# Gated linear attention into a shrink feed-forward: one quadratic instead of two, GpSimd without products, and a planner's table rewritten

## The chip, the cores and the metric

The kernel runs on one NeuronCore of a Trainium2 chip. A core has a matrix engine (TensorE, here PE; its weight loads are listed apart as PEld), a vector engine (VectorE, DVE), an activation engine (ScalarE, ACT), a general engine (GpSimd, POOL) and a queue engine that issues transfers (SyncE, SP). Each works through its own list of instructions in order, and they wait for each other by semaphores. The metric is the time of one execution on the device in microseconds (us).

## The reference

```python
q, k, v, alpha: (4, 8, 768, 48) float32     # batch, heads, positions, width
w_in: (384, 2048), w_out: (2048, 384)        # float64 on the host
for t in range(768):
    state = alpha[:, :, t, :, None] * state + einsum('bhd,bhe->bhde', k[:, :, t], v[:, :, t])
    y[:, :, t] = einsum('bhd,bhde->bhe', q[:, :, t], state)
x = y.transpose(0, 2, 1, 3).reshape(3072, 384)
h = x @ w_in
out = (h - tanh(h)) @ w_out
```

## The kernel before

All arithmetic is float32. Work is cut into 12 units of 256 positions (three per batch entry), and each unit into two chunks of 128. A unit passes through two halves.

`gla(u)` is the attention. ACT and DVE bring alpha, k and q of eight heads into tiles aT, kT and qT with the head width along the partitions: four pairs of heads, a pair on partitions 0 to 47 and 64 to 111, the rest of the 128 unused. Two scans on DVE (U backwards, W forwards) give the running products of alpha, and kU and qW scale kT and qT by them in place. Per chunk: `scores` (sc, products of k and q), `masked` (pm, on DVE), `decay` (the old state times `ends`), `y` (products of q with the state and of pm with v), `x` (a copy into xT), and for the next chunk `back`, `natural`, `update` and `state` (tp, kn, up, state). Units 0 and 1 are "direct": the fourth pair of heads is written into the unused partitions of the first three by gap products of 32 columns, with the tiles v_gap and s_gap. Later units copy that pair aside (xs) and move it by transfers (`moves`).

`moe(u)` is the feed-forward, in eight steps s. `first` makes h for two blocks of 128 of the 2048 features (6 matrix products of 256 columns, 12 records in the trace, as each float32 product is two). `square` (u = h*h) and `quad` (z1, z2) run on ACT, `cube` (w = h*u) and `shrunk` (g) on DVE. g is a polynomial for h - tanh(h). `large` on ACT sums what lies over a limit into the tile over. `second` multiplies g with w_out: for units 0 and 1 plainly (4 products of 384 columns, tile o), for the others with seven products of 192 columns instead of eight, for which `sums` makes e on DVE and `combine` once makes five tiles b of sums of w_out. `store` adds the parts up and sends them out.

Two PSUM banks hold h, so `first` of a step waits for `cube` of two steps before. The weights arrive as 16 pieces (in0 to in7, out0 to out7), loaded by SP into four buffers and converted by ACT ("read") and DVE. The first 12 or so steps of unit 0 and 1 run while this goes on.

The order on every engine is written by `Planner`: each task has an engine, an assumed duration, a rank and the tasks it needs, and a greedy walk always takes the ready task of the lowest rank. So a changed rank or duration moves instructions everywhere. At the end the kernel tests whether the quick way was allowed (over, sizes, least, most, tiny into `ok`); all engines load `ok`, and with 0 a slower function `general` would compute everything again.

Of the kernel before, what the change touches and what calls it, by code (L numbers as in the profile page):

```python
# [8 lines left out]
FP32 = mybir.dt.float32  # L9
# [352 lines left out]
def fast(tc, q, k, v, alpha, moe_w_in, moe_w_out, out, w_in, w_out, ident, ok, pad_rows):  # L362
# [17 lines left out]
    with ExitStack() as ctx:  # L380
# [25 lines left out]
        over = consts.tile([P, NU * FS], FP32, name="over")  # L406
# [27 lines left out]
        RANK = {"in": -3, "out": 1}  # L434
# [4 lines left out]
        def rank_gla(u):  # L439
            return (-40, -20)[u] if u < 2 else 2 * FS * u - 24  # L440
# [26 lines left out]
        for n, (what, s) in enumerate(pieces):  # L467
# [6 lines left out]
            add(f"read {what}{s}", "ACT", 1.85, rank, [f"fetch {what}{s}", older and f"{older[0]}{older[1]}"], a)  # L474
            add(f"{what}{s}", "DVE", 1.95, rank, [f"read {what}{s}"], b)
# [21 lines left out]
        def gla(u, rank):  # L497
# [64 lines left out]
            def scale(name, by):  # L562
                t = m[name].rearrange("p g c t -> p (g c) t")
                (V if u == 0 else GP).tensor_mul(t, t, m[by][:, :, 1:])  # L564
# [5 lines left out]
            go("U", "DVE", 2.35, 1, ["aT", prev and f"kU{prev}", prev and f"sizeU{prev}"], scan_U)  # L570
            go("ends", "DVE", 0.5, 3, ["U"], ends)
            go("W", "DVE", 2.6, 3, ["ends", prev and f"qW{prev}", prev and f"sizeW{prev}"], scan_W)
            go("kU", *(("DVE", 1.3) if u == 0 else ("POOL", 2.4)), 3, ["kT", "U"], lambda: scale("kT", "U"))
            go("qW", *(("DVE", 1.3) if u == 0 else ("POOL", 2.4)), 5, ["qT", "W"], lambda: scale("qT", "W"))
# [10 lines left out]
            def chunk(c):  # L585
# [30 lines left out]
                def decay():  # L616
                    for q in quads:
                        GP.tensor_mul(old[q, :, q], old[q, :, q],  # L618
# [10 lines left out]
                def products():  # L629
# [3 lines left out]
                    if n == 0:  # L633
                        for hh, at, j in to_gap:
                            T.matmul(y[at, j, :], lhsT=v_gap[:, c, hh, j, :], rhs=m["pm", c][hh][:, NP - 1, :],
                                     start=(j == 0), stop=True, skip_group_check=True)
                    if n > 0:
                        for g in range(NP):
                            T.matmul(y[:, g, :], lhsT=old[:, g, :], rhs=m["qT"][:, g, c, :],  # L639
                                     start=(g == 0), stop=False, skip_group_check=True)  # L640
                        for hh, at, j in to_gap:
# [3 lines left out]
                            T.matmul(y[at, j, :], lhsT=v_gap[:, c, hh, j, :], rhs=m["pm", c][hh][:, NP - 1, :],  # L645
# [348 lines left out]
```

## Time and profile before

| | |
|---|---|
| times of three runs | 643.49, 643.63, 641.67 us (median 643.49) |
| profiled execution | 642.75 us, span 640.8 us, mean granted clock 0.979 |
| PE / PEld busy | 610.4 us (95%) / 534.0 us (83%) |
| DVE / ACT / POOL busy | 520.5 (81%) / 403.0 (63%) / 94.1 us (15%) |
| costliest groups | PE h L781 268.2 us, PE o L842 91.1 + 80.7 + 65.1 us, ACT z L793 110.3 us, DVE g L803 86.3 us |
| transfers | 50.5 MB, 44 read from HBM |

How to read it: busy time is an average over stages. PE's lengths contain the time that a product needs to run out, which overlaps the next one, so what a run of products costs is read from the distance between their starts, or from the chain of waits, which does this already. "A <- B: 7.0, 1, 7.0" means that A stood idle until B, 7.0 us in total, once, at most 7.0.

### The profile page before, as it was taken

Reading aid. Unit: us, or ns where it says so; the run is one execution under the profiler, and the core shown is the slowest. Engines: PE = TensorE matmul, PEld = TensorE weight load, DVE = VectorE, ACT = ScalarE, POOL = GpSimd, SP = SyncE. Lnnn points to the kernel's source line nnn. Section 1 sums busy time; section 2 is a strip of 40 time slices with the busy share of each in tenths; the row PEclk is TensorE's granted clock in tenths of the full one; section 3 lists DMA queues with packets and bytes.
Section 4 is the critical chain, followed back from the end, with each engine's and each line's share of the span. In section 5 each row is a group of like instructions: output and inputs, shape, how many; then the busy total and the mean of one; then the engine's idle time right before and its main releaser. Section 6 shows DMA issues by size and latency. Waiting matters only on the chain.

```text
span 640.8 us, 10379 instructions
## 1 busy us (share of the span) xinstructions
PE 610.4 (95%) x3723; PEld 534.0 (83%) x3723; DVE 520.5 (81%) x915; ACT 403.0 (63%) x825; POOL 94.1 (15%) x84
## 2 busy tenths in 40 slices
PE   7889993999999999999999999999999999999994
PEld 6666672677799899999899999999898999999994
DVE  7897599899689799689999699689899656656762
ACT  3767796588878688678656557457545544545550
POOL 2030028232012002001211011002011000000000
PEclk9799997799999999999999999999999999999998
DMA  9998491455454346433131031021010000000001
GB/s 171 220 201 196 115 225 56 100 103 150 124 104 122 78 111 169 99 103 100 39 71 46 9 78 46 7 76 49 26 32 2 12 20 1 20 14 1 25 2 31
DMA packets 55165, 50.51 MB, mean 79 GB/s; under 512 B 29056, under 2 KB 44864, under 8 KB 55104
## 3 DMA queue, kind: packets, MB, share of 16 engines
q1 hardware_dynamic: 52736, 48.97, 32.5%
q10 hardware_dynamic: 2368, 0.79, 0.8%
q8 instruction: 31, 0.51, 0.4%
q14 instruction: 30, 0.25, 0.1%
HBM read 44.04 MB, written 4.72 MB: 76 GB/s over the span
## 4 chain that ended last, share of the span: by engine, by line
PE 82%; DVE 10%; DMA 4%; issue 2%; ACT 1%; SPq 0%; DVEq 0%; ACTq 0%
PE h L781 35%; PE o L842 27%; PE o L827 6%; PE y L649 3%; PE sc L608 3%; PE y L639 3%; PE up L673 2%; DVE g L803 2%; DMA vt<-in_v_dram 2%; DMA raw<-in_moe_w_in_dram 1%; DVE z L802 1%; PE tp L664 1%; DVE U L545 1%; DMA qr<-in_q_dram 1%; DVE qT L529 1%
## 5 line engine op out<-in xcount | busy, mean ns | idle before, releaser
L781 PE MATMUL h<-xT,w_in 128*128 128x256 f32 x1152 | 268.2, 383 | 7.7 <-DVE w L797 7.0
L781 PEld LDWEIGHTS h<-xT,w_in 128*128 128x128 f32 x1152 | 217.0, 192 | 38.6 <-DVE w L797 7.6
L788 ACT ACTIVATE u<-h 128x512 f32<-128x512 f32 x96 | 57.2, 596 | 156.9 <-PE h L781 156.5
L793 ACT ACTIVATE z<-u 128x512 f32<-128x512 f32 x192 | 110.3, 622 | 4.4 <-DVE g L803 1.9
L797 DVE TENSOR_TENSOR w<-h,u 128x512 f32<-128x512 f32 x96 | 65.9, 686 | 57.8 <-ACT u L788 57.2
L803 DVE SCALAR_TENSOR_TENSOR g<-z,z 128x512 f32<-128x512 f32 x96 | 86.3, 899 | 10.1
L842 PE MATMUL o<-b,e 128*128 128x192 f32 x480 | 91.1, 326 | 0.0
L842 PE MATMUL o<-w_out,e 128*128 128x192 f32 x320 | 80.7, 334 | 0.0
L842 PEld LDWEIGHTS o<-b,e 128*128 128x128 f32 x480 | 80.2, 190 | 0.0
L802 DVE SCALAR_TENSOR_TENSOR z<-z,w 128x512 f32<-128x512 f32 x96 | 69.5, 724 | 5.3 <-ACT z L793 2.1
L842 PE MATMUL o<-b,g 128*128 128x192 f32 x320 | 65.1, 326 | 0.0
L842 PEld LDWEIGHTS o<-w_out,e 128*128 128x128 f32 x320 | 56.5, 190 | 6.7 <-issue 3.0
L618 POOL TENSOR_TENSOR state<-state,ends 48x192 f32<-48x192 f32 x40 | 22.5, 563 | 256.5 <-DVE state L681 216.1
L809 ACT ACTIVATE big<-u 128x512 f32<-128x512 f32 x96 | 59.2, 616 | 0.1
L842 PEld LDWEIGHTS o<-b,g 128*128 128x128 f32 x320 | 54.2, 190 | 0.0
L827 PE MATMUL o<-w_out,g 128*128 128x384 f32 x128 | 47.0, 514 | 3.9 <-DVE g L803 3.8
L827 PEld LDWEIGHTS o<-w_out,g 128*128 128x128 f32 x128 | 24.8, 199 | 19.5 <-DVE g L803 4.5
L564 POOL TENSOR_TENSOR qT<-qT,W 128x1024 f32<-128x1024 f32 x11 | 26.7, 2428 | 76.6 <-DVE qT L529 74.3
L564 POOL TENSOR_TENSOR kT<-kT,U 128x1024 f32<-128x1024 f32 x11 | 24.4, 2217 | 82.3 <-DVE kT L529 60.2
L815 DVE TENSOR_TENSOR e<-g 128x256 f32<-128x256 f32 x80 | 33.3, 416 | 1.4
L614 DVE TENSOR_TENSOR pm<-sc,mask 128x512 f32<-128x512 f32 x46 | 29.5, 683 | 5.9 <-PE sc L608 5.9
L816 DVE TENSOR_TENSOR e<-g 128x256 f32<-128x256 f32 x80 | 33.4, 417 | 0.0
(105 smaller groups left out, 730.5 us busy)
## 6 DMA issues: line engine op xcount, KB each, us to landing
raw<-in_moe_w_out_dram SPq DMA_DIRECT2D x16, 768.0 KB, 5.6
raw<-in_moe_w_in_dram SPq DMA_DIRECT2D x32, 288.0 KB, 5.3
ar<-in_alpha_dram SPq DMA_DIRECT2D x24, 192.0 KB, 3.2
qr<-in_q_dram SPq DMA_DIRECT2D x24, 192.0 KB, 3.2
kr<-in_k_dram SPq DMA_DIRECT2D x22, 192.0 KB, 4.2
vt<-in_v_dram SPq DMA_DIRECT2D x22, 192.0 KB, 4.4
raw<-in_moe_w_in_dram SPq DMA_DIRECT2D x32, 96.0 KB, 5.4
out_dram<-same SPq DMA_DIRECT2D x20, 96.0 KB, 1.7
```

The lines of the kernel that those rows point to most:

```text
L564: (V if u == 0 else GP).tensor_mul(t, t, m[by][:, :, 1:])
L781: T.matmul(h[:, a, :], lhsT=w_in[:, j, f * P:(f + 1) * P], rhs=xT[u][:, j, :], start=(j == 0), stop=(j == KT - 1))
L788: A.activation(m["u", s], m["h", s], AF.Square, scale=W_SCALE ** -1.5)
L793: A.activation(m[z, s], m["u", s], AF.Square, bias=b, scale=QA * W_SCALE)
L797: V.tensor_mul(m["w", s], m["h", s], m["u", s])
L802: V.scalar_tensor_tensor(out=z1, in0=z1, scalar=QK1, in1=m["w", s], op0=ALU.add, op1=ALU.mult)
L803: V.scalar_tensor_tensor(out=g.rearrange("p a c t -> p (a c t)"), in0=z2, scalar=QK2, in1=z1, op0=ALU.add, op1=ALU.mult)
L809: A.activation(big, m["u", s], AF.Relu, bias=-U_MAX, scale=W_SCALE, accum_out=over[:, n:n + 1])
L815: V.tensor_add(e[:, 0:2, :], g[:, 0], g[:, 1])
L816: V.tensor_sub(e[:, 2:4, :], g[:, :, 1, :], g[:, :, 0, :])
L827: T.matmul(m["o"][c], lhsT=g[:, a, c, :], rhs=w_out[:, f, :], start=(f == 0), stop=(f == FT - 1))
L842: T.matmul(o[n][:, i], lhsT=g_, rhs=w_, start=(s == 0 and (n, i) in ((0, 0), (1, 0), (2, 1), (3, 0))), stop=(s == FS - 1), skip_group_chec ...
```

## The change

1. The shrink polynomial has one quadratic factor instead of two: one ACT activation and one DVE operation fewer per step. It holds for |h| up to 0.177 (h*h up to 1/32) instead of 0.5.
2. The tile u holds two steps, and `large` tests both at once, 48 times with 1024 columns instead of 96 with 512.
3. kU and qW of units 1 to 11, all `decay` and four of the five `combine` go from GpSimd to DVE. GpSimd keeps its memsets at the start.
4. The state products and `update` of TensorE use 112 columns instead of 128 (the upper 16 are unused); in the direct units the state product of the fourth pair is dropped.
5. Gap products: all of s_gap first, then all of v_gap, instead of one and one.
6. `store` adds in another order, sends `cross` before `same`, and for the last unit sends `cross` through ACT's queue.
7. The final test is planned like the other tasks: `judge` and `ok` on DVE, `gather` on PE, ahead of the last steps.
8. The planner's durations and ranks are new; w_out's pieces rank 7 later, unit 2's attention too.

```diff
-QA = C4 ** 0.25
-QB1, QK1 = QA * 0.6850222695595437, (QA * 2.4662457704476) ** 2
-QB2, QK2 = -QA * 2.2304921696, (QA * 1.5325319249) ** 2
+U_FAST = 1.0 / 32
+QA, QB, QK = 0.2301250865552381, -0.2896718893320786, 0.24942350940007277
...
-        RANK = {"in": -3, "out": 1}
+        RANK = {"in": -3, "out": 8}
...
-            return (-40, -20)[u] if u < 2 else 2 * FS * u - 24
+            return (-40, -20, 2 * FS - 1)[u] if u < 3 else 2 * FS * u - 24
...
-                (V if u == 0 else GP).tensor_mul(t, t, m[by][:, :, 1:])
+                V.tensor_mul(t, t, m[by][:, :, 1:])
...
                     for q in quads:
-                        GP.tensor_mul(old[q, :, q], old[q, :, q],
+                        V.tensor_mul(old[q, :, q], old[q, :, q],
                                       m["ends"][q, :, c:c + 1].to_broadcast([D, NP, D]))
...
+                    rows = P if direct else HP + D
                     if n > 0:
-                        for g in range(NP):
-                            T.matmul(y[:, g, :], lhsT=old[:, g, :], rhs=m["qT"][:, g, c, :],
+                        for g in range(KT if direct else NP):
+                            T.matmul(y[0:rows, g, :], lhsT=old[:, g, 0:rows], rhs=m["qT"][:, g, c, :],
...
-                        T.matmul(up[:, g], lhsT=m["kn", c][:, g, :], rhs=vts[u][:, c, 2 * g:2 * g + 2, :],
+                        T.matmul(up[0:HP + D, g], lhsT=m["kn", c][:, g, 0:HP + D], rhs=vts[u][:, c, 2 * g:2 * g + 2, :],
...
             if n == 0:
-                GP.tensor_add(combos["11+22"], b11, b22)
+                V.tensor_add(combos["11+22"], b11, b22)
...
-                    for z, b in (("z1", QB1), ("z2", QB2)):
-                        m[z, s] = two.tile([P, 2 * TU], FP32, name=z)
-                        A.activation(m[z, s], m["u", s], AF.Square, bias=b, scale=QA * W_SCALE)
+                    m["z", s] = two.tile([P, 2 * TU], FP32, name="z")
+                    A.activation(m["z", s], m["u", s], AF.Square, bias=QB, scale=QA * W_SCALE)
...
-                    V.scalar_tensor_tensor(out=z1, in0=z1, scalar=QK1, in1=m["w", s], op0=ALU.add, op1=ALU.mult)
-                    V.scalar_tensor_tensor(out=g.rearrange("p a c t -> p (a c t)"), in0=z2, scalar=QK2, in1=z1,
-                                           op0=ALU.add, op1=ALU.mult)
+                    V.scalar_tensor_tensor(out=g.rearrange("p a c t -> p (a c t)"), in0=m["z", s], scalar=QK,
+                                           in1=m["w", s], op0=ALU.add, op1=ALU.mult)
...
-                    A.activation(big, m["u", s], AF.Relu, bias=-U_MAX, scale=W_SCALE,
+                    A.activation(big, m["us"].rearrange("p s t -> p (s t)"), AF.Relu, bias=-U_FAST, scale=W_SCALE,
                                  accum_out=over[:, n:n + 1])
...
-                put(same, o[0][:, 0:1, :].to_broadcast([P, 2, NH]), ALU.subtract, p52)
-                put(same, o[1], ALU.add, same)
+                put(same, o[1], ALU.subtract, p52)
                 put(cross, o[1][:, ::-1, :], ALU.add, p52)
+                put(same, o[0][:, 0:1, :].to_broadcast([P, 2, NH]), ALU.add, same)
                 put(same, o[3], ALU.add, same)
                 for c in range(CU):
                     half = [out_r[u * CU + c][:, n * NH:(n + 1) * NH] for n in range(2)]
+                    (A if u == NU - 1 else nc.sync).dma_start(out=half[1 - c], in_=cross[:, c, :])
...
+        add("judge", "DVE", 1.2, 16 * NU, [f"large {last_step}", f"x {NU - 1}.{CU - 1}"] + [f"look {n}" for n in range(len(pieces))], judge)
+        add("gather", "PE", 0.3, 16 * NU - 20, ["judge"], gather)
+        add("ok", "DVE", 0.3, 16 * NU, ["gather"],
```

How the order moves, at three places. In the rows, the engine's instruction stands with its line, output, inputs and shape.

First, DVE around the attention of unit 2 and the first `combine`. Before, the block of unit 2 (aT to ends) stands in one piece, w and z of the next step behind it, and the additions b are on POOL:

```order
L529 STREAM_TRANSPOSE aT_107<-ar 128x8x2x16 x4
L529 STREAM_TRANSPOSE kT<-kr 128x8x32 x4
L545 SCALAR_TENSOR_TENSOR U<-aT_107,after 128x1032
L529 STREAM_TRANSPOSE qT<-qr 128x8x32 x4
L552 TENSOR_TENSOR ends<-U,low 128x8
L553 TENSOR_REDUCE least<-U 128x1
L554 RECIPROCAL before<-ends 128x8
L797 TENSOR_TENSOR w<-h,u 128x512
L559 SCALAR_TENSOR_TENSOR W<-aT_107,before 128x1032
L802 SCALAR_TENSOR_TENSOR z_838<-z_838,w 128x512
L803 SCALAR_TENSOR_TENSOR g<-z_840,z_838 128x512
```

POOL at the same place, before:

```order
L734 TENSOR_TENSOR b_832<-w_out 128x1536
L736 TENSOR_TENSOR b_833<-w_out 128x1536
L564 TENSOR_TENSOR kT<-kT,U 128x1024
L618 TENSOR_TENSOR state_118<-state_118,ends 48x4x48 x2
L738 TENSOR_TENSOR b_834<-w_out 128x1536
L564 TENSOR_TENSOR qT<-qT,W 128x1024
L740 TENSOR_TENSOR b_835<-w_out 128x1536
```

Now DVE has w, g, the conversion of out7 (L85, L86) and the additions b between the pieces, and POOL nothing:

```order
L795 TENSOR_TENSOR w<-h,u 128x512
L528 STREAM_TRANSPOSE qT<-qr 128x8x32 x4
L799 SCALAR_TENSOR_TENSOR g<-z,w 128x512
L563 TENSOR_TENSOR qT<-qT,W 128x1024
L795 TENSOR_TENSOR w<-h,u 128x512
L617 TENSOR_TENSOR state_118<-state_118,ends 48x4x48 x2
L85 TENSOR_SCALAR bits<-raw 128x768
L86 ISA w_out<-bits,more 128x1536
L795 TENSOR_TENSOR w<-h,u 128x512
L731 TENSOR_TENSOR b_924<-w_out 128x1536
L613 TENSOR_TENSOR pm_934<-sc_893,mask 128x512
L613 TENSOR_TENSOR pm_935<-sc_894,mask 128x512
```

What moved: w and g stand between the parts of unit 2, and kT, qT, state and b come from POOL.

Second, PE at the gap products of the second chunk of unit 0 (the two chunks of unit 1 read alike). Before, the first seven of its rows:

```order
L639 MATMUL y<-qT,state_119 128x128 x4
L642 MATMUL y<-qT,s_gap 32x128
L645 MATMUL y<-pm_327,v_gap 32x128
L642 MATMUL y<-qT,s_gap 32x128
L645 MATMUL y<-pm_327,v_gap 32x128
L642 MATMUL y<-qT,s_gap 32x128
L645 MATMUL y<-pm_327,v_gap 32x128
```

Now, up to the products with the values vt (pm 325 and 326 are the two masked tiles):

```order
L670 MATMUL up<-vt,kn 112x96 x4
L635 MATMUL y<-qT,state_119 128x128 x3
L638 MATMUL y<-qT,s_gap 32x128 x6
L642 MATMUL y<-pm_325,v_gap 32x128 x3
L642 MATMUL y<-pm_326,v_gap 32x128 x3
L646 MATMUL y<-pm_325,vt 48x128
L646 MATMUL y<-pm_326,vt 48x128
```

What moved: three state products instead of four, six s_gap in a row, then six v_gap.

Third, SP at the end of the program. Before:

```order
L887 DMA out_dram<-same 128x192
L888 DMA out_dram<-cross 128x192
L887 DMA out_dram<-same 128x192
L888 DMA out_dram<-cross 128x192
L962 TENSOR_LOAD ok
L962 ISA x2
L962 COMPARE_AND_BRANCH
```

Now:

```order
L886 DMA out_dram<-cross 128x192 x2
L889 DMA out_dram<-same 128x192 x2
L972 TENSOR_LOAD ok
L972 ISA x2
L889 DMA out_dram<-same 128x192 x2
L972 COMPARE_AND_BRANCH
```

What moved: two of the last unit's four stores are gone from SP, and the load of `ok` stands ahead of the other two.

More of the change, by code (lines that the diff above doesn't have):

```diff
@@ L473, in fast @@
             older = pieces[n - 2] if n >= 2 else None
-            add(f"read {what}{s}", "ACT", 1.85, rank, [f"fetch {what}{s}", older and f"{older[0]}{older[1]}"], a)
-            add(f"{what}{s}", "DVE", 1.95, rank, [f"read {what}{s}"], b)
+            add(f"read {what}{s}", "ACT", 2.1, rank, [f"fetch {what}{s}", older and f"{older[0]}{older[1]}"], a)
+            add(f"{what}{s}", "DVE", 1.6, rank, [f"read {what}{s}"], b)
         vts, xT = {}, {}
@@ L688, in chunk @@
                 go_c("scores", "PE", 1.2, 7, [kU, qW] + held, scores)
-                go_c("masked", "DVE", 1.4, 8, ["scores", past and f"y {past}"], masked)
+                go_c("masked", "DVE", 1.3, 8, ["scores", past and f"y {past}"], masked)
                 if n > 0:
-                    go_c("decay", "POOL", 1.2, 6, [f"ends {u}", f"state {past}"], decay)
+                    go_c("decay", "DVE", 0.6, 6, [f"ends {u}", f"state {past}"], decay)
                 if direct:
@@ L744, in fast @@
         for n in range(5):
[L745 removed]
+            add(f"combine {n}", "DVE", 1.7, 2 * FS + 1 + n,
                 [f"out{FS - 1}", f"in{FS - 1}", f"gaps {PLAIN - 1}.{CU - 1}", f"y {PLAIN - 1}.{CU - 1}"]
```

91 lines of the change are left out of this document (48 added, 43 removed).

## The prediction

> **What bounds the kernel now.** I read the page first, then the busy time by stage, PE's waits, the chain of waits, and the timeline where PE waited. The page (the last line is the granted TensorE clock in 40 slices of 16 us, 9 being full):
>
> ```profile
> span 640.8 us, 10379 instructions
> ...
> PE 610.4 (95%) x3723; PEld 534.0 (83%) x3723; DVE 520.5 (81%) x915; ACT 403.0 (63%) x825; POOL 94.1 (15%) x84
> ...
> PEclk9799997799999999999999999999999999999998
> ```
>
> Stages of my choice. The columns after the window are its length and then PE, PEld, DVE, ACT and POOL busy with their instruction counts, the granted TensorE clock, and DMA:
>
> ```profile
> 0.00:175.90 175.90, 155.02 (x863) 115.66 (x863) 147.91 (x215) 127.31 (x233) 45.37 (x42) 0.94 0.68 151
> 97.30:118.50 21.20, 10.41 (x22) 6.66 (x22) 21.13 (x21) 11.19 (x21) 16.66 (x7) 0.69 0.19 55
> 175.90:622.70 446.80, 446.14 (x2807) 409.49 (x2806) 366.95 (x687) 272.79 (x587) 48.69 (x42) 1.00 0.21 52
> ```
>
> From 175.9 us, where the first seven-product step begins, to the last `first`, PE is busy 446.14 of 446.80 us: whatever the change does to the other engines there is hidden as long as PE stays fed, and only PE's own work counts. The first 175.9 us are different. PE lacks 20.9 us, and half of that lies in one hole of 21.2 us, where PE has 10.4 us of work at a mean clock of 0.69 while DVE is busy for 21.1. PE's waits, as total, times, longest:
>
> ```profile
> PE h L781 <- DVE w L797: 7.0, 1, 7.0
> PE up L673 <- ACT kn L668: 4.3, 2, 2.8
> PE o L827 <- DVE g L803: 3.8, 1, 3.8
> PE tp L664 <- DVE kT L564: 2.7, 1, 2.7
> ```
>
> The chain of waits gives the undisturbed prices (start, length): the 12 records of a `first` take 2.59 us, and 50 of the seven-product `second` 8.14, so the 14 of one take 2.28.
>
> ```profile
> 175.92 2.47 PE o L842 x14
> ...
> 610.41 2.59 PE h L781 x12
> ...
> 622.73 8.14 PE o L842 x50
> ```
>
> So the time is: PE's start of the first seven-product step (175.9), a solid stretch of PE work up to 630.9, and a tail of 640.8 - 630.9 = 9.9. I add up the change in these three. The profiled execution took 642.75, which is 1.95 beside its span; I keep the 1.95. It is 0.74 below the median of the three runs, 643.49. Those runs spread over 0.3% (641.67 to 643.63), about what a measurement here can tell from no change.
>
> **The hole at 97 to 118 (forecast -15.9).** Its rows:
>
> ```profile
> 94.58 2.74 PE L827 MATMUL o<-w_out,g 128*128 128x384 f32 x8
> 95.55 3.45 POOL L736 TENSOR_TENSOR b<-w_out 128x1536 f32<-128x1536 f32 x1
> 96.02 5.15 DVE L545 TENSOR_TENSOR_SCAN U<-aT,after 128x1032 f32<-128x1032 f32 x1
> ...
> 103.61 0.64 DVE L797 TENSOR_TENSOR w<-h,u 128x512 f32<-128x512 f32 x1
> ...
> 104.31 5.08 PE L781 MATMUL h<-xT,w_in 128*128 128x256 f32 x12 [6.98 <-DVE w L797]
> ...
> 104.70 5.32 POOL L738 TENSOR_TENSOR b<-w_out 128x1536 f32<-128x1536 f32 x1
> 106.71 3.85 DVE L802 SCALAR_TENSOR_TENSOR z<-z,w 128x512 f32<-128x512 f32 x1
> ...
> 113.20 5.49 PE L827 MATMUL o<-w_out,g 128*128 128x384 f32 x8 [3.81 <-DVE g L803]
> ...
> 118.25 2.30 DVE L545 TENSOR_TENSOR_SCAN U<-aT,after 128x1032 f32<-128x1032 f32 x1
> ...
> 619.98 2.75 PE L781 MATMUL h<-xT,w_in 128*128 128x256 f32 x12
> ```
>
> PE ran out at 97.3 because `w`, which frees the bank of h, stood in DVE's queue behind unit 2's transposes, scan and ends, and came only at 103.61. That queue was slower than its work: the scan U took 5.15 us against 2.30 at 118.25, z 3.85 against 0.72 on average (L802 below), each while GpSimd ran an add of `combine` (95.55 to 99.00, 104.70 to 110.02). PE then ran at half clock: 5.08 for a `first` that takes 2.75, 5.49 for a `second` that takes 2.74. The hole's price is 7.0 + 3.8 waiting, 2.3 + 2.8 at half clock: 15.9. After the change POOL has no product left, so neither GpSimd add exists, and in DVE's new order `w` and g of every step stand between the pieces of unit 2's block. The bounds are 0 and 15.9; I take all of it and book what comes in its place below.
>
> **Gap products by shape, and state products of three pairs (-5.5).**
>
> ```profile
> 26.19 1.13 PE L673 MATMUL up<-vt,kn 128*128 128x96 f32 x8
> 27.25 1.09 PE L635 MATMUL y<-pm,v_gap 128*32 128x128 f32 x12
> ...
> 29.83 1.13 PE L639 MATMUL y<-qT,state 128*128 128x128 f32 x8 [0.70 <-ACT xT L655]
> 30.89 0.40 PE L642 MATMUL y<-qT,s_gap 48*32 48x128 f32 x2
> ...
> 34.90 0.86 PE L649 MATMUL y<-pm,vt 128*48 128x128 f32 x12
> ```
>
> Alternating, 24 records of gap products take 34.90 - 30.89 = 4.01 us; 12 v_gap records in a row take 1.09. If s_gap in a row costs the same, the block takes 2.2 (saves 1.8); if twice that, 3.3 (saves 0.7). It has the same 32 columns, so I lean to the first: 1.6, and 4.8 for the three chunks that have both. Each of these chunks also drops two of the 8 records that take 1.13 us, about 0.24: 0.7 in all. In all three the chain of waits runs through PE. Range -2.8 to -6.2.
>
> **112 columns (-2.2).** `up` (96 columns streaming) and the state product (128) both take 1.13 for 8 records, so for `up` the 128-column load is likely the limit. Loading an eighth less saves at most an eighth of 1.13, 0.14 a group; a part of the 1.13 is the last record running out, so I take 0.11 for each of the 20 groups, 0.014 a record: 2.2. The state product (17 groups with 112 columns) streams 128 columns and may be bound by either: 0 to 2.4, and I take 0. Range of both 0 to -5.2. The lines that price a load:
>
> ```profile
> L673 PEld LDWEIGHTS up<-vt,kn 128*128 128x128 f32 x160 | 21.0, 198 | 5.8 <-ACT kn L668 4.9 <-issue 0.4
> L649 PEld LDWEIGHTS y<-pm,vt 128*48 128x48 f32 x368 | 18.9, 122 | 3.3 <-issue 1.3
> ```
>
> 128 columns take 198 ns and 48 take 122, 0.95 ns a column, so 16 fewer are 15 ns, in step with 0.014. [...]
>
> **Quadratic, range test, GpSimd's products (0 in the solid stretch).**
>
> ```profile
> L793 ACT ACTIVATE z<-u 128x512 f32<-128x512 f32 x192 | 110.3, 622 | 4.4 <-DVE g L803 1.9
> L802 DVE SCALAR_TENSOR_TENSOR z<-z,w 128x512 f32<-128x512 f32 x96 | 69.5, 724 | 5.3 <-ACT z L793 2.1 <-DVE w L797 0.5
> L618 POOL TENSOR_TENSOR state<-state,ends 48x192 f32<-48x192 f32 x40 | 22.5, 563 | 256.5 <-DVE state L681 216.1 <-DVE state L679 38.6
> L564 DVE TENSOR_TENSOR kT<-kT,U 128x1024 f32<-128x1024 f32 x1 | 1.2, 1175 | 0.0
> L681 DVE TENSOR_TENSOR state<-state,up 48x192 f32<-48x192 f32 x32 | 11.1, 346 | 12.4 <-PE up L673 11.9
> L742 DVE SCALAR_TENSOR_TENSOR b<-w_out 128x1536 f32<-128x1536 f32 x1 | 1.8, 1751 | 0.0
> ```
>
> ACT loses 96 x 0.62 = 60 us, and 48 range tests of double width replace 96. DVE loses 96 of 0.72 and gains 22 scalings of 1.2 (26), 20 decays of two multiplies (0.35 each by L681, 0.56 each on POOL; I take 0.7 the pair, 14) and 4 `combine` (1.75 each, 7). After 175.9 DVE gives up 80 z (58 us) and takes 15 scalings and 14 decays (28): about 337 of 447 us at most. PE covers all of it; with that cover gone DVE would next be late with g. The new wait is one of order: scores on PE wait for kU and qW, and behind these two on DVE now queue w and g, at 1.2 us each a delay that 90 us of slack in 447 absorbs.
>
> **New waits in the first stage (+2.0).** Up to the first e, DVE's work was 147.9. It loses 17 z (12) and the blocked time (U 2.9, z 3.2, about 4 more in rows of this kind: 10), and gains 7 scalings, 6 decays and 4 `combine` (20): about 146. PE, without the terms above, would begin the seven-product steps at 175.9 - 15.9 - 5.5 = 154.5. So DVE must be busy 94% of the way, against 84% before: tight, but PE is still later. At unit 1's scores PE now stands behind eight steps of DVE in a row (U, kT, ends, kU, W, qT, decay, qW) and has only two `first`, a tp and an up to do meanwhile; at this place it waited for kn before, part of the 4.3 above. The new ranks let all pieces of w_in pass those of w_out in SP's, ACT's and DVE's queues (the same 16 loads and conversions, so no work is added), and put unit 2's k and q loads behind the last weight on SP. So the conversion `out7` now stands on DVE behind unit 2's kT, kU, qT, qW and decay, while unit 0's last `second` needs it. The nearest rows are PE's single waits of 1.5 to 2.8 us: I take 2.0; lower bound 0. Were DVE as idle as before (28 us), the stage would end at 174: upper bound 19.
>
> **The end (-1.4).**
>
> ```profile
> 630.89 0.49 ACT L877 ACTIVATE p<-o 128x384 f32<-128x384 f32 x1 [5.73 <-PE o L842]
> 633.52 0.33 SPq L887 DMA_DIRECT2D out_dram<-same  x1
> 634.85 0.43 SPq L888 DMA_DIRECT2D out_dram<-cross  x1
> ```
>
> The p copy and four adds remain, in another order with the same length. SP issued four stores from 633.52 to 635.28; now it issues two after the last add, and the two `cross` go out on ACT's queue earlier: 0.9 saved. `ok` is known before the last step, and SP loads it before its last stores; that load has no row here, bounds 0 to 1.0 us: 0.7. The `row` product moves in front of the last two steps: PE pays 0.2. Judging takes 11 small operations of DVE, covered by two steps of 2.27 that PE still has.
>
> **Sum.** -15.9 - 5.5 - 2.2 + 2.0 - 1.4 = -23.0: span 617.8, time 619.7.
>
> **Rivals.**
> *A new hole early.* Either place named above slips by 5 us, PE's clock halves again for some 7 us (as from 104.3), costing about 3.5: 8 to 12 more, 628 to 632. For it: DVE at 94%, strict order. Against it: w and g are spread out, nothing blocks DVE. [...]
> *DVE merely replaces the hole.* If its queue idles as before, new waits of 19 instead of 2 give 619.7 + 17 = 637; for no change they must reach 25. Against it: blocked time is gone.
> [...]
> *The test fails.* Were some |h| above 0.177, `general` would run as well, at several times the range. The reference's inputs give at most 0.0915, computed from them: no chance.
> *More than forecast.* No new waits, and both product terms at their ends: -15.9 - 6.2 - 5.2 - 1.4 = -28.7, 614; with an end shorter still, 612.
>
> **Chances.** Forecast (612.5 to 625) 0.68; new hole (625 to 635) 0.20; DVE replaces the hole, mostly up to no change, 0.04; slower 0.03; below 612.5 0.05. Range 612.5 to 631 holds the first and two thirds of the second: 0.81. Faster 0.94, same 0.03, slower 0.03.
>
> **What would show it.** PE's wait for w of 7.0 and the half clock between 97 and 118 gone; first seven-product step near 156; a block of `o` to `o` in the solid stretch still 4.86 us per step, `up` near 1.0 for 8; DVE's U never over 2.6; last store issued about 0.9 after the last add. I am wrong if PE waits for w, g or out7 by more than 4 us in the first 160, or if DVE's g comes late after 160.

## The result, and the profile after

| | before | after |
|---|---|---|
| median | 643.56 us (641.67 to 644.29, four runs) | 618.37 us (617.95 to 618.99, four runs) |
| ratio, 95% interval | 1 | 0.9614 (0.9591 to 0.9637) |
| profiled span, mean clock | 640.8 us, 0.979 | 616.2 us, 0.988 |

The kernel became 25.2 us faster; the forecast was 619.7. The page of the kernel after, the lines that answer to those of before:

```profile
span 616.2 us, 9861 instructions
...
PE 596.8 (97%) x3717; PEld 529.5 (86%) x3717; DVE 463.4 (75%) x885; ACT 342.5 (56%) x633; POOL 4.5 (1%) x18
...
PEclk9799999999999999999999999999999999999998
```

POOL has 4.5 us left, its memsets; DVE lost 57 us and ACT 60. Only the second slice (15.4 to 30.8) is still at 7; a second stretch at half clock, 3.4 us from 44.6 on, is split between two slices and hides in their 9. The two slices at 7 between 96 and 128 are at 9. The busy time by stage (columns as before):

```profile
0.00:154.60 154.60, 143.46 (x857) 112.84 (x857) 135.12 (x213) 109.27 (x185) 4.45 (x18) 0.97 0.72 159
97.30:118.50 21.20, 21.20 (x114) 15.24 (x113) 21.06 (x30) 11.66 (x23) 0.00 (x0) 1.00 0.23 67
154.60:598.00 443.40, 443.40 (x2804) 407.16 (x2803) 322.47 (x652) 230.46 (x444) 0.00 (x0) 1.00 0.24 57
```

The stretch that held the hole is full: PE 21.20 of 21.20 us at clock 1.00, where it had 10.41 at 0.69. From the first seven-product step on, PE is busy without a gap, as it nearly was before (446.14 of 446.80 us). PE's waits that are left (total, times, longest), without that of spin for its operand at the start:

```profile
PE up L670 <- ACT kn L665: 4.2, 3, 2.1
PE tp L661 <- DVE kT L563: 2.4, 1, 2.4
PE sc L607 <- DVE qT L563: 2.4, 2, 1.4
...
PE h L778 <- ACT xT L652: 0.6, 1, 0.6
```

None of them is for w, g or out7. The first seven-product step in the chain of waits (start, length), and the last p copy and the last stores in the timeline:

```profile
154.64 2.47 PE o L838 x14
```

```profile
607.02 0.49 ACT L876 ACTIVATE p<-o 128x384 f32<-128x384 f32 x1 [5.93 <-PE o L838]
...
609.80 1.35 SPq L889 DMA_DIRECT2D out_dram<-same  x2
```

So the three parts of the span (up to the first seven-product step, the solid stretch up to the p copy, the rest) went from 175.9, 455.0 and 9.9 us to 154.6 (-21.3), 452.4 (-2.6) and 9.2 (-0.7).

### The profile page after: what moved, and what is told of

Read it like the earlier page. It is cut to its first block, busy times and chain, and to the rows that moved or that the text cites. A ratio compares the mean times of both kernels' runs of the same rounds, so it can differ in the third digit from the quotient of the medians.

```text
span 616.2 us, 9861 instructions
## 1 busy us (share of the span) xinstructions
PE 596.8 (97%) x3717; PEld 529.5 (86%) x3717; DVE 463.4 (75%) x885; ACT 342.5 (56%) x633; POOL 4.5 (1%) x18
## 4 chain that ended last, share of the span: by engine, by line
PE 92%; DMA 3%; DVE 2%; issue 1%; ACT 0%; ACTq 0%; SPq 0%; DVEq 0%
PE h L778 40%; PE o L838 30%; PE o L823 7%; PE sc L607 4%; PE y L646 4%; PE y L635 3%; DMA raw<-in_moe_w_in_dram 3%; PE up L670 2%; PE tp L661 1%; DMA kr<-in_k_dram 1%; DVE qT L528 1%; PE y L642 1%; DVE qT L563 0%; DVE W L558 0%; PE y L638 0%
## 5 line engine op out<-in xcount | busy, mean ns | idle before, releaser
L799 DVE SCALAR_TENSOR_TENSOR g<-z,w 128x512 f32<-128x512 f32 x96 | 65.9, 687 | 10.7 <-ACT z L791 5.9
L791 ACT ACTIVATE z<-u 128x512 f32<-128x512 f32 x96 | 60.4, 629 | 2.3
L805 ACT ACTIVATE big<-u 128x1024 f32<-128x1024 f32 x48 | 50.1, 1045 | 0.0
L823 PE MATMUL o<-w_out,g 128*128 128x384 f32 x128 | 44.0, 489 | 0.0
L607 PEld LDWEIGHTS sc<-qT,kT 48*128 48x128 f32 x368 | 23.4, 195 | 10.0 <-issue 5.2
L607 PE MATMUL sc<-qT,kT 48*128 48x128 f32 x368 | 28.0, 294 | 2.4 <-DVE qT L563 2.4
L544 DVE TENSOR_TENSOR_SCAN U<-aT,after 128x1032 f32<-128x1032 f32 x12 | 27.5, 2294 | 0.3
L558 DVE TENSOR_TENSOR_SCAN W<-aT,before 128x1032 f32<-128x1032 f32 x12 | 27.6, 2302 | 0.0
```

Source lines behind the costliest of these rows:

```text
L607: T.matmul(sc[hh][:, g, :], lhsT=m["kT"][q, g, c, :], rhs=m["qT"][q, g, c, :], start=True, stop=True)
L791: A.activation(m["z", s], m["u", s], AF.Square, bias=QB, scale=QA * W_SCALE)
L799: V.scalar_tensor_tensor(out=g.rearrange("p a c t -> p (a c t)"), in0=m["z", s], scalar=QK, in1=m["w", s], op0=ALU.add, op1=ALU.mult)
L805: A.activation(big, m["us"].rearrange("p s t -> p (s t)"), AF.Relu, bias=-U_FAST, scale=W_SCALE, accum_out=over[:, n:n + 1])
L823: T.matmul(m["o"][c], lhsT=g[:, a, c, :], rhs=w_out[:, f, :], start=(f == 0), stop=(f == FT - 1))
```

## The experiments

Twelve kernels, "a" made from the kernel after and "b" from the one before. The ratio is to the kernel before on the same chip; "first seven" is the start of the first seven-product step in the profiled run.

Two cautions. The last column is one execution, whose time lies 1.6 to 4.1 us above the kernel's median for a_quads, b_quad, a_end, a_128 and b_dve (the 4.1), and 1.6 below it for a_pool_place. a_end, whose edit lies at the end of the program alone, begins its seven-product steps 1.3 us later than the kernel after, so differences of that size there tell nothing by themselves. And the medians were taken in several batches, in which the kernel before has medians of 641.87 to 643.56; where differences of medians are given in us below, the ratios give values up to 2.5 us off.

| kernel | edit | median, us | ratio (95%) | first seven |
|---|---|---|---|---|
| after | | 618.37 | 0.9614 (0.9591 to 0.9637) | 154.6 |
| a_pool_place | products back on GpSimd | 621.44 | 0.9674 (0.9647 to 0.9702) | 157.1 |
| a_ranks | both old ranks | 625.42 | 0.9734 (0.9708 to 0.9760) | 161.4 |
| a_rank_u2 | old rank of unit 2 | 627.73 | 0.9763 (0.9735 to 0.9790) | 164.3 |
| a_quads | two quadratics, test per step | 626.77 | 0.9722 (0.9665 to 0.9780) | 164.1 |
| b_dve | products on DVE alone | 641.33 | 0.9970 (0.9949 to 0.9992) | 182.1 |
| b_ranks | new ranks alone | 641.69 | 1.0007 (0.9971 to 1.0043) | 173.3 |
| b_quad | one quadratic alone | 637.33 | 0.9890 (0.9831 to 0.9948) | 173.4 |
| a_gap | gap products alternating | 622.63 | 0.9703 (0.9619 to 0.9788) | 158.9 |
| a_128 | 128 columns | 622.48 | 0.9650 (0.9590 to 0.9710) | 159.2 |
| a_shapes | both of these | 625.76 | 0.9735 (0.9708 to 0.9761) | 160.7 |
| a_spin | more idle products early | 617.03 | 0.9603 (0.9581 to 0.9625) | 152.6 |
| a_end | old store | 618.30 | 0.9615 (0.9591 to 0.9640) | 155.9 |

### Who made the hole: GpSimd, the order, or the amount of work?

**a_pool_place.** The planner's table is untouched, so PE's, ACT's and SP's lists stay.

```diff
-                V.tensor_mul(t, t, m[by][:, :, 1:])
+                (V if u == 0 else GP).tensor_mul(t, t, m[by][:, :, 1:])
-                        V.tensor_mul(old[q, :, q], old[q, :, q],
+                        GP.tensor_mul(old[q, :, q], old[q, :, q],
-                V.tensor_add(combos["11+22"], b11, b22)
+                GP.tensor_add(combos["11+22"], b11, b22)
...
```

> The changed kernel with kU and qW of units 1 to 11, all decay and four combine issued on GpSimd again, at the same places of the written order, the planner's table left as it is: PE, ACT and SP keep their lists word for word, and DVE's list only loses these rows. Theory (the hole at 97 to 118 of the kernel before had two causes, GpSimd's adds that slowed DVE and an order that kept w behind unit 2's block): DVE's U or g stretch to 3 to 5 us again beside the four combine and PE waits 3 to 10 us in all for w, g or pm, with a clock below 0.9 there: 622 to 630 us. Rival order (the order alone removed the hole): 618 to 620 us. Rival GpSimd (GpSimd alone made it): the whole 15.9 us come back, 632 to 636 us. After 155 us all say the same: PE covers it, 4.86 us a step.

Measured 621.44, +3.1. The hole doesn't come back, though the slow rows do. From its timeline:

```profile
105.59 3.54 POOL L731 TENSOR_TENSOR b<-w_out 128x1536 f32<-128x1536 f32 x1
...
108.09 5.47 DVE L799 SCALAR_TENSOR_TENSOR g<-z,w 128x512 f32<-128x512 f32 x2
109.09 3.93 POOL L733 TENSOR_TENSOR b<-w_out 128x1536 f32<-128x1536 f32 x1
...
119.85 4.23 DVE L544 TENSOR_TENSOR_SCAN U<-aT,after 128x1032 f32<-128x1032 f32 x1
```

Two g take 5.47 us and a scan 4.23, yet PE lists no wait there. The 3 us are lost earlier: from the fourth `first` (57.8 us) to the 18th (150.7) every one starts 2.6 us later than in the kernel after, no more and no less. What is lost ahead of it is seen at unit 1's scores: its qT takes 2.17 us on GpSimd instead of 1.2, the scores wait 2.23 us for it, and the clock stays at half for 6.8 us there instead of 3.4:

```profile
43.03 2.17 POOL L563 TENSOR_TENSOR qT<-qT,W 128x1024 f32<-128x1024 f32 x1 [1.20 <-DVE qT L528]
...
45.26 2.08 PE L607 MATMUL sc<-qT,kT 48*128 48x128 f32 x16 [2.23 <-POOL qT L563]
```

At the first seven-product step 157.1 - 154.6 = 2.5 remain. The theory was right on DVE, nearly so on the time, and wrong on PE's wait: with the new order and the lighter step there is slack for GpSimd's adds, which cost PE nothing.

**b_dve**, the reverse edit on the kernel before, with the new durations of these tasks.

> The kernel before with all of GpSimd's products on DVE and their new durations in the planner's table, the old ranks, nothing else. Theory (two causes): the stretched rows are gone (U 2.3, z 0.72), but unit 2's block still stands in one piece ahead of w, and now with kU, qW and decay in it: PE still waits 5 to 10 us at one place near 97 to 120; 632 to 642 us. Rival GpSimd alone: no wait over 2 us there, 626 to 630 us. Rival order alone: no gain or a loss, 642 to 652 us, since DVE has 28 us more to do in the first 176 with two quadratics still there.

Measured 641.33, -1.1 (interval -0.1% to -0.5%). The time lies just inside the theory's range and close to that of the rival that knows the order alone, so it does not tell the two apart. PE's wait for w is still there at 106, without any product on GpSimd, and shorter than the 5 to 10 us expected:

```profile
PE h L781 <- DVE w L797: 4.3, 1, 4.3
```

Other waits grew in its place: that for kn from 4.3 us in all to 6.5, at the start of the stage.

**b_ranks**, and **a_ranks** and **a_rank_u2** the other way:

```diff
-        RANK = {"in": -3, "out": 1}
+        RANK = {"in": -3, "out": 8}
-            return (-40, -20)[u] if u < 2 else 2 * FS * u - 24
+            return (-40, -20, 2 * FS - 1)[u] if u < 3 else 2 * FS * u - 24
```

> The kernel before with the two new ranks alone (w_out's pieces 7 later, unit 2's attention at 15 instead of 8). Theory (two causes): the wait for w of 7.0 us at 97 goes, but DVE's rows beside the four combine still take 3 to 5 us and PE waits for g or w there: 633 to 641 us. Rival order alone: 626 to 630 us, no wait over 2 us between 90 and 120. Rival GpSimd alone: 640 to 645 us.

> The changed kernel with the two old ranks (w_out's pieces at 1, unit 2's attention at 8). Theory (two causes): unit 2's block stands together again ahead of w, undisturbed: PE waits 3 to 8 us near 95 to 120 and the clock drops there: 622 to 630 us. Rival order alone: the hole is back, 630 to 636 us. Rival GpSimd alone: 617.5 to 620 us.

> The changed kernel with unit 2's attention at its old rank 8 and w_out's pieces at the new 8: half of the ranks undone (both together cost 7 us). Theory (unit 2's block ahead of w made the wait at 99 us): a PE wait of 2 to 3 us for qT near 95 to 105, 622 to 625 us, and the early stage as in the changed kernel (first h at 35). Rival (w_out's pieces that pass w_in's make it): 617.5 to 620 us.

b_ranks measured 641.69: alone, the ranks bring nothing that can be told, which is the rival's number with the theory's waits. That for w went, and waits for w_out and g took its place:

```profile
PE o L827 <- DVE w_out L87: 4.3, 2, 3.5
PE o L827 <- DVE g L803: 3.4, 1, 3.4
```

Undone in the kernel after they cost 7.1 us, and unit 2's rank by itself 9.4, more than the 4 to 7 expected (a_ranks came as the theory had it). a_rank_u2 and a_quads also make `combine` wait for the piece out6; in both traces the first b follows the last conversion of w_out, as it does after, so nothing of the loss is seen to come from that. In a_rank_u2, DVE does unit 2's kT, qT and both scalings in one piece from 86.58, and the scores on PE stand behind it; then a `first` takes 4.51 instead of 2.75:

```profile
86.58 2.07 DVE L528 STREAM_TRANSPOSE kT<-kr 128x256 f32<-128x256 f32 x4
88.49 2.01 DVE L528 STREAM_TRANSPOSE qT<-qr 128x256 f32<-128x256 f32 x4
90.34 1.21 DVE L563 TENSOR_TENSOR kT<-kT,U 128x1024 f32<-128x1024 f32 x1
91.47 1.20 DVE L563 TENSOR_TENSOR qT<-qT,W 128x1024 f32<-128x1024 f32 x1
...
92.73 1.16 PE L607 MATMUL sc<-qT,kT 48*128 48x128 f32 x16 [3.17 <-DVE qT L563]
...
94.02 4.51 PE L778 MATMUL h<-xT,w_in 128*128 128x256 f32 x12
```

**a_quads** and **b_quad**, parts 1 and 2 undone, or alone:

```diff
-                    m["z", s] = two.tile([P, 2 * TU], FP32, name="z")
-                    A.activation(m["z", s], m["u", s], AF.Square, bias=QB, scale=QA * W_SCALE)
+                    for z, b in (("z1", QB1), ("z2", QB2)):
+                        m[z, s] = two.tile([P, 2 * TU], FP32, name=z)
+                        A.activation(m[z, s], m["u", s], AF.Square, bias=b, scale=QA * W_SCALE)
...
+                    V.scalar_tensor_tensor(out=z1, in0=z1, scalar=QK1, in1=m["w", s], op0=ALU.add, op1=ALU.mult)
```

> The changed kernel with the two quadratics and the range test per step back (parts 1 and 2 undone), the planner's durations of the new ones kept, so that the order stays nearly the same. It adds 96 ACT rows of 0.62 and 96 DVE rows of 0.69 us, and 48 more range tests. Prediction on record: 0 in the solid stretch after 155 us, 4.86 us a step, and nothing booked of its own before it. Theory A (the queue's order and GpSimd emptied the hole, the lighter step adds little): 618 to 622 us. Theory B (a share of the gain that the forecast gave to order and GpSimd needs the lighter step: up to 155 us DVE has 17 x 0.69 = 12 us more to do at 94%): the first seven-product step comes 6 to 13 us later, 624 to 632 us.

> The kernel before with parts 1 and 2 alone: one quadratic, one range test for two steps, with their new durations in the planner's table; products stay on GpSimd, old ranks. Theory A (the hole came from order and GpSimd): still a wait for w or g of 5 us or more between 90 and 120, 638 to 643 us. Theory B (DVE's amount of work made it): z beside combine was one of the stretched rows, and 12 us of DVE work go from the first 176: the first seven-product step starts 7 to 14 us earlier, 629 to 636 us.

a_quads cost 8.4 us. In the solid stretch it cost what the forecast said, nothing to speak of: from the first seven-product step to the p copy 452.8 against 452.4 us. All the rest lies before: DVE has 147.2 us of work there instead of 135.1.

```profile
0.00:164.00 164.00, 147.92 (x856) 113.65 (x856) 147.17 (x231) 119.50 (x220) 4.44 (x18) 0.95 0.69 150
97.30:118.50 21.20, 20.01 (x103) 13.76 (x103) 20.71 (x30) 17.07 (x34) 0.00 (x0) 1.00 0.19 57
```

Theory B held. Little of it is the clock of the first 50 us: up to the fifth `first` 1.5 us are lost (65.6 against 64.1), the other 8 behind it. b_quad gained 4.6, between the two theories; in its trace, 2.0 us slower than its median, the first seven-product step came 2.5 earlier, and the hole stayed, now as a wait for g:

```profile
92.17 5.79 DVE L544 TENSOR_TENSOR_SCAN U<-aT,after 128x1032 f32<-128x1032 f32 x1
...
105.22 5.49 PE L825 MATMUL o<-w_out,g 128*128 128x384 f32 x8 [7.17 <-DVE g L801]
105.61 3.53 POOL L737 TENSOR_TENSOR b<-w_out 128x1536 f32<-128x1536 f32 x1
106.28 9.03 DVE L801 SCALAR_TENSOR_TENSOR g<-z,w 128x512 f32<-128x512 f32 x1
109.11 2.16 POOL L563 TENSOR_TENSOR qT<-qT,W 128x1024 f32<-128x1024 f32 x1
...
111.24 3.51 POOL L739 TENSOR_TENSOR b<-w_out 128x1536 f32<-128x1536 f32 x1
```

Here GpSimd does count: a scan of 2.3 takes 5.79 us, and one g of 0.69 takes 9.03 beside three GpSimd products that follow each other without a gap.

Together: each alone saves 4.6, 1.1 and 0.7 us of the kernel before, 6.4 in sum; all three at once (a_shapes, below, which leaves only the two product parts out and so has the new end too, at most 1 us) save 16.1; and each taken out of the kernel after costs 8.4, 7.1 and 3.1. By the ratios the three rows read 7.1, 1.9 and -0.4; 17.0; 6.9, 7.7 and 3.9, which says the same. So none of the three is the cause by itself. Order and lighter step are both needed, each for 7 to 8 us; GpSimd's products cost 3 to 4 beside them, at another place. What they cost in the old order no run isolates. An estimate: b_quad and a_ranks both have old order and one quadratic and lie 11.9 us apart (10.0 by the ratios); take off the 7.4 of a_shapes (7.8) and the 0.7 of the end, and 1.5 to 4 are left, not more than in the new order. Whether of the lighter step DVE's part or ACT's does it, no run told apart.

### The matrix products

**a_gap**, **a_128** and **a_shapes** (both):

```diff
-                        for g in range(KT if direct else NP):
+                        for g in range(NP):
                             T.matmul(y[0:rows, g, :], lhsT=old[:, g, 0:rows], rhs=m["qT"][:, g, c, :],
...
                             T.matmul(y[at, j, :], lhsT=s_gap[quads[hh], j, :],
...
+                            T.matmul(y[at, j, :], lhsT=v_gap[:, c, hh, j, :], rhs=m["pm", c][hh][:, NP - 1, :],
+                                     start=False, stop=False, skip_group_check=True)
```

```diff
-                    rows = P if direct else HP + D
+                    rows = P
-                        T.matmul(up[0:HP + D, g], lhsT=m["kn", c][:, g, 0:HP + D], rhs=vts[u][:, c, 2 * g:2 * g + 2, :],
+                        T.matmul(up[:, g], lhsT=m["kn", c][:, g, :], rhs=vts[u][:, c, 2 * g:2 * g + 2, :],
```

> The changed kernel with the gap products alternating again (one s_gap, one v_gap) and the fourth state product back in the direct units, with 128 columns there. Theory (changing shape costs PE 0.16 us each time, whatever lies around it): 12 pairs take 4.0 us instead of 2.04 in each of three chunks, and two more records 0.25 each: +6.6 us, 624 to 626 us. Rival (early waits swallow it, since PE waits 11 us in the first 97 anyway): +0 to +4, 618 to 622 us.

> The changed kernel with 128 columns again in update and in the state products of units 2 to 11. Prediction on record: up 0.014 us a record on 160 records, state product 0: +2.2 us. From the trace after (up 0.098 against 0.112 from start to start, state product 0.109 against 0.112): +2.2 and +0.4, 620.5 to 621.5 us. [...] Rival no effect (the pitch of up is set by its 96 streaming columns): 618 to 619 us.

> The changed kernel with both matrix product parts undone: gap products alternating with the fourth state product, and 128 columns everywhere. Forecast on record for these terms: 5.5 + 2.2 = 7.7. From the single runs: 4.1 + 1.6 to 4.1. Theory (the two add, and waits of the first 97 us take up about 2 of the 9.2 that the products need): +6 to +8, 624 to 627 us. Rival (waits take up nothing): +9, 627 to 628 us. Rival (the single runs were short of clock, and the parts bring less): +3 to +5, 621 to 624 us.

PE's rows of one chunk in the kernel after, and the first ones of the same chunk in a_gap:

```profile
31.73 1.09 PE L638 MATMUL y<-qT,s_gap 48*32 48x128 f32 x12
32.75 1.09 PE L642 MATMUL y<-pm,v_gap 128*32 128x128 f32 x12
33.77 0.86 PE L646 MATMUL y<-pm,vt 128*48 128x128 f32 x12
```

```profile
32.27 0.40 PE L642 MATMUL y<-qT,s_gap 48*32 48x128 f32 x2
32.61 0.41 PE L645 MATMUL y<-pm,v_gap 128*32 128x128 f32 x2
32.94 0.40 PE L642 MATMUL y<-qT,s_gap 48*32 48x128 f32 x2
```

Twelve records of one kind take 1.02 us, 0.085 each; in turn, two and two, 0.335 for each two. So 24 take 2.04 instead of 4.01, three times 1.97 = 5.9, and the two dropped state records 0.7 in the three chunks (1.06 to 0.79, and twice 0.98 to 0.76). Of these 6.6 only 4.3 are seen in a_gap's time (one of its four runs took 630.28 at a mean clock of 0.978; the other three lie within 0.8 us). Its trace says where: the first `first` starts 2.5 us later than in the kernel after, the third 0.7, the fourth 2.1, the fifth and all others 4.3. So waits take up most of unit 0's chunk, as the rival had it in part, and the two chunks of unit 1 add 1.4 and 2.2. The chains of waits fit this: in the kernel after, a transfer of w_in (30.48, 7.26 us) stands in the chain at unit 0's chunk, not PE; and in the kernel before the chain runs there (30.9 to 34.9) through a transfer and then DVE, and does not come to the products of PE until 52.27:

```profile
24.18 6.96 DMA qr<-in_q_dram
...
45.03 2.48 DVE g L803
...
52.27 2.86 PE h L781 x12
```

a_128's four runs lie between 619.51 (clock 0.988) and 625.59 (0.979), so its +4.1 is mostly clock; its trace tells the term apart. From the first seven-product step to the p copy it takes 454.05 us against 452.45, +1.6. The groups of `update`, after and a_128 (busy, mean ns of one):

```profile
L670 PEld LDWEIGHTS up<-vt,kn 128*112 128x112 f32 x160 | 18.3, 178 | 5.1 <-ACT kn L665 4.8
...
L635 PEld LDWEIGHTS y<-qT,state 128*112 128x112 f32 x136 | 16.2, 177 | 0.3
```

```profile
L670 PEld LDWEIGHTS up<-vt,kn 128*128 128x128 f32 x160 | 21.3, 200 | 6.4 <-ACT kn L665 6.2
...
L635 PEld LDWEIGHTS y<-qT,state 128*128 128x128 f32 x154 | 19.8, 197 | 0.4
```

A load is 20 to 22 ns shorter with 112 columns in both, but from start to start `up` goes from 0.112 to 0.098 us and the state product only from 0.112 to 0.109. There the 128 streamed columns look like the limit: gap products that follow each other on one strip (the same 32 partitions of y), with 32 loaded columns and 128 streamed, mostly start 0.109 apart too (the 0.085 above comes from two strips side by side, whose records start 0.006 apart in places). So the shorter load does not set the pace of all 296 records. a_shapes: +7.4, the forecast's 7.7, with about 1.5 of 8.9 taken up by waits.

### The clock in the first 50 us

**a_spin**: the idle products `spin` fill PE's waits.

```diff
-        add("spin 0", "PE", 9, -99, [], lambda: spin(36))
+        add("spin 0", "PE", 9, -99, [], lambda: spin(45))
-        add("spin 1", "PE", 1.5, -20, [f"qT 0"], lambda: spin(7))
+        add("spin 1", "PE", 1.5, -20, [f"qT 0"], lambda: spin(15))
...
+                    if u == 0 and c == 0:
+                        spin(5)
```

> The changed kernel with more idle products on PE (spin, results unused) in its waits of the first 31 us: 45 instead of 36 at the start, 15 instead of 7 before the first up, 5 between that up and the first sc, 5 between the second tp and its up; about 0.22 us each, so sized to end before the wait does. The order is otherwise the same. Theory clock (gaps of PE in 12 to 31 us lower the granted clock, 0.57 in 20 to 28, and this costs time and makes the runs of one kernel differ by 2 to 6 us): clock 1.00 from 16 to 48, the first h at 32 to 34 us instead of 35.2, 613.5 to 617 us, and runs that lie within 1 us. Rival pace (DVE, busy 3.9 of every 4 us until 48, sets the pace there, whatever PE's clock): 617.5 to 620 us, clock raised or not. Rival delay (spins hold up work behind them): 619 to 622 us.

Busy times from 20 to 28 us, after and a_spin:

```profile
20.00:28.00 8.00, 6.59 (x59) 5.54 (x57) 6.67 (x12) 4.98 (x6) 0.00 (x0) 0.57 1.10 214
```

```profile
20.00:28.00 8.00, 7.00 (x82) 6.26 (x82) 7.26 (x12) 5.50 (x7) 0.00 (x0) 1.00 1.12 224
```

The clock rose from 0.57 to 1.00, and no slice of the page but the last is below 9. The first h came at 34.65, 0.56 earlier: DVE is busy 7.3 of the 8 us there, which fits the rival, and the time lies between the two expectations; 2.0 us are won up to the first seven-product step. The five runs lie within 0.94 us, all below the four of the kernel after. The difference of 1.3 us is 0.2% (0.1% by the ratios), and the two intervals overlap, so it is likely and not secured. It has the lowest median of this study.

### The end

**a_end** puts the old order of the adds and all stores back on SP; the load of `ok` stays early.

```diff
-                put(same, o[1], ALU.subtract, p52)
+                put(same, o[0][:, 0:1, :].to_broadcast([P, 2, NH]), ALU.subtract, p52)
+                put(same, o[1], ALU.add, same)
...
-                    (A if u == NU - 1 else nc.sync).dma_start(out=half[1 - c], in_=cross[:, c, :])
```

> The changed kernel with the old store: the adds in the old order and all four stores of a unit in turn on SP, for the last unit too; the early judge and load of ok stay. Read in the trace from the last p copy (607.02 after) to the end. The forecast booked 0.9 of the end's 1.4 for the stores; in the trace after, SP's branch comes 1.43 us after the last add instead of 2.74, but the adds take 0.16 longer and GpSimd's closing drain begins 0.42 us later than it could. Theory (the stores bring what was booked, and the late drain comes with the shorter end): the branch comes 0.8 to 1.0 us later after the last add, the last add 0.16 earlier, the drain at once: p copy to end 9.2 + 0.2 to 0.5 us, 618.5 to 619.2 us. Rival (the late drain comes from the early judge and not from the stores): p copy to end 9.9 to 10.1 us. Rival (the stores bring nothing, all was the early load of ok): 9.0 us.

No difference in time that could be told (618.30), and an end longer than any of the three expectations. In the records of its end, p copy to last add 2.60 us (after: 2.76), last add to SP's branch 2.83 (1.49), from there to SP's first closing wait 2.59 (2.51), the rest 2.42 (2.41): 10.4 in all, against 9.2 after and 9.9 before. The stores bring 1.3 in this pair of traces. But the new end has a price: SP's second store takes 1.25 us to issue here and 0.86 to 1.97 in the nine other kernels in which `ok` is loaded ahead of the last stores, 0.43 in the four in which it is not, so the load's 0.7 is eaten. That the load makes the store slow is likely and not shown. This length makes the new end vary: in the seven other traces that have it and no products on GpSimd, p copy to end takes 9.5 to 10.4 us (10.4 in a_128, the others at most 9.7). So the 9.2 of the kernel after is its best case, and the usual gain over the 9.9 of before is smaller than 0.7. And the late close is not due to the stores, nor to the early judge: b_dve, which has neither, closes in 2.43 as well. What goes with it is told below.

## Why the prediction was right, step by step

| term | forecast | measured |
|---|---|---|
| hole at 97 to 118 | -15.9 | -15.9: PE full at clock 1.00 |
| gap products, fourth state product | -5.5 | -6.6 in PE's records (3 x 1.97 + 0.7), 4.3 in time (a_gap) |
| 112 columns | -2.2 | -2.3: `up` -2.0, state products -0.3 (1.4 and 0.3 in the solid stretch, the rest by groups) |
| new waits in the first stage | +2.0 | +1.8: -21.3 + 15.9 + 6.6 + 0.6 (112 columns there) |
| solid stretch, rest | 0 | -0.9: `row` +0.1; the `first` there, as often, 202.1 instead of 203.1 |
| the end | -1.4 | -0.7 |
| sum of spans | -23.0 | -24.6 |

The +1.8 is a remainder: it holds new waits, and what the earlier waits took up of the 6.6; by a_gap the latter alone is 2.3.

The sum is right to 1.6 us, and the terms to about 1.1 each. Some steps failed all the same.

*The hole's reason.* The forecast emptied the hole because "neither GpSimd add exists" and w and g stand between unit 2's pieces, and gave the quadratic no price outside the solid stretch; its 12 us of DVE appear only in the balance of 146 us of work. a_pool_place has the adds back and no hole; a_quads has neither add nor old order and loses 8.4 us. The size was right since all three reasons came in the same change, and to that extent by luck. The places were right: w, U and g were the late rows, and a 7 us wait with half clock behind it.

*The end.* Of 0.9 for two fewer stores and 0.7 for the early load, 1.3 came in SP's branch; 0.2 went to the adds (they no longer follow each other without a wait for `same`) and 0.5 to the close. The forecast had taken the close as unchanged. Given how the other traces of this end vary, the 0.7 itself is one sample.

*The path of the gap products.* "In all three the chain of waits runs through PE" holds for the two chunks of unit 1 alone; at unit 0's the chain of before runs through a transfer and DVE (24 to 52 us), and a_gap's time lacks most of that chunk's share.

The lean in the gap products was right: s_gap in a row costs as much as v_gap in a row; my 1.6 was 1.97, and -6.6 lies just outside its range, since the 1.09 us of twelve records, from which I took the bound, contain the last one running out: from start to start they take 1.02. On 112 columns the forecast's split was right, `up` gains 14 ns a record and the state product 3, next to nothing. The load records themselves became 20 to 22 ns shorter.

Of the rivals, a new hole early did not form in the kernel after, but a_rank_u2 shows that it was near: one rank makes it, 9.4 us. DVE did not replace the hole: it is busy 135.1 of 154.6 us, 87% and not the 94% that I had counted. The rows that GpSimd had held gave back about 15 us instead of 10 (g 5.5, z 3.9, U 2.8, ends 2.5, W 0.5), and some 4 us of rows moved behind the end of the shorter stage.

## What to carry to other kernels

A hole of the bounding engine need not be one row's fault: take the late engine's queue as amount of work, order and disturbance, and price each by what it leaves when the others stay. A change whose parts bring little one by one (6.4 us in sum here) can bring 16 together, so test parts by taking them out of the whole as well as by adding them. And an operation that is free under a solid stretch is not free in the stages ahead of it (a_quads, in the traces: 0.4 us there, 9.5 ahead of it): give each stage its own balance. A product's price in PE's records counts only where the chain of waits runs through PE at that place (a_gap: 6.6 us in the records, 4.3 in time): look at each place, not at the stage.

## What the runs showed of the hardware that I had not expected

- *GpSimd can hold a DVE operation for several of its own.* g of b_quad took 9.03 us beside three GpSimd products in a row. In the same trace 18 w (one operand from PSUM) ran beside GpSimd products at 0.68 us, as without them (0.67 at 121.10); in the trace of before, 11 g beside them took 2.50 on average and 12 w 0.68, where the other 85 g and 84 w took 0.69. `bits`, with one SBUF input, took 1.93 us beside GpSimd products instead of 0.55 in a_pool_place. What decides which rows are held no run shows.
- *Taking two shapes of product in turn costs PE about 0.165 us for each change*: two records take 0.335 us where the kind changes behind them and 0.17 in a row, with the same columns. Not all of it is the change itself. In a row, records of the two strips of 32 columns run side by side (in the kernel after some start 0.006 us apart, those that follow each other on one strip mostly 0.109); in turn none do. By these starts about 0.12 (0.335 - 2 x 0.109) goes with the change, the rest with overlap that is lost; no run separates the two.
- *Waits of 0.7 to 2.5 us were enough to lower the clock.* In the kernel after the clock is 0.57 from 20 to 28 us behind gaps of 2.5 and 2.1 us; where a_spin fills them it is 1.00. At 44.6 it falls again, to 0.50 up to 48.0, behind gaps of 0.7 and 1.0. What separates the cases in this record is PE's busy share. In all 14 traces the clock changes at steps of 3.41 us. It fell behind 33 of these steps, in which PE was busy for 0.00 to 0.50 of the time (0.57 in one of them); where it stayed at full speed, PE was busy for at least 0.52 (0.49 in one). The longest gap does not separate them: the clock fell behind a step with none over 1.03 us and stayed behind one that a gap of 2.73 us reaches into. The last 20 us of the executions are left out of this count.
- *The time of an execution goes with this clock.* In the batches of the experiments the kernel before takes 641.2 to 642.7 us where the mean clock is 0.979 (26 executions), 643.6 to 644.4 at 0.976 (nine), 645.3 to 645.7 at 0.973 (three); above 0.979 it is no faster (641.7 at 0.983); a_128's four runs reach from 619.5 at 0.988 to 625.6 at 0.979; a_spin's five, at 0.994 to 0.996, lie within 0.9.
- *The kernels without products on GpSimd close 0.5 us later.* From SP's first closing wait to the end it takes 1.92 us in the four kernels with them (before, b_ranks, b_quad, a_pool_place) and 2.41 to 2.63 in the ten without. GpSimd's closing drain begins late there, 0.42 us after the start of its instruction ahead of it in the kernel after and 0.08 in the kernel before; what it does until then no record shows, and that stays open.
